# State attention and a gated projection on one core: parity tiles for the scores, and a new order of issue

## The chip, the cores and the metric

The kernel runs on one core of a Trainium2 chip. The core has five engines that each work through their own instructions in order: TensorE (PE in the rows; its weight loads are listed apart as PEld), VectorE (DVE), ScalarE (ACT), GpSimd (POOL) and SyncE (SP), which here issues all DMAs. They meet at semaphores. Matmuls write to PSUM, which this kernel uses as eight banks of 128x512 fp32; everything else lies in SBUF. The metric is the device time of one execution in microseconds.

## The reference

```
# B, H, S, Ns, D = 8, 8, 512, 32, 64; all arrays fp32 (the weights are float64 at the door)
scores  = x @ state.T / sqrt(D)          # (B, H, S, Ns): softmax over the states
xread   = softmax(scores) @ state
scores2 = state @ x.T / sqrt(D)          # (B, H, Ns, S): softmax over the tokens
sread   = softmax(scores2) @ x
seq     = concat([xread, sread], tokens) # (B, S + Ns, H * D)
gate    = sigmoid(causal depthwise conv of seq, 5 taps)
out     = (gate * (seq @ w_val)) @ w_out # (B, 576, 512)
```

Both softmaxes use the same scores, once along the states and once along the tokens.

## The kernel before

There are eight batches. For one batch the kernel loads x, transposes it on PE in four pieces (`xTp`, copied to `xT`), and multiplies with the scaled transposed state: `sc` holds in two PSUM banks, one for each g, the scores of 4 heads by 32 states on the 128 partitions against 512 tokens. DVE transposes `sc` in 32x32 blocks (`scores_T`) and goes on with the softmax over the states there: `max_n`, `sub_n`, `exp_n` on ACT, `sum_n`, `scale_n`, and a transpose back (`probs`). The softmax over the tokens is a max per partition (`max_s`) and an exponential with a summed output on ACT (`exp_s`), transposed on PE (`e2p`) and multiplied with x (`srp`). The probabilities then meet the state twice: `xr` (the read, which only the gate uses; batch 0 does the convolution on PE, the others as taps on DVE) and `val`, the read already multiplied with w_val (`sgv`, split in a high and a low half `swh`, `swl`, as are the probabilities, `ah`, `al`). `g` is gate times value on DVE, split into `gh` and `gl`; `op` is the projection with w_out, 12 matmuls of 128x128x512 for each of four token groups, and `tail` does the 32 state rows of all batches at the end (`tval`, `tacc`, `tg`, `top`). Weights arrive as 64-bit words and are converted by the `words_` functions (`wv`, and `ws_o` for w_out).

Batches 0, 1 and 2 (`LONG`) load x in runs of four tokens, 1 KB at a time: a partition holds tokens 4p to 4p+3 of a head, and a transpose takes two of them at a time, so partitions 0 to 63 of `xT` hold even tokens and 64 to 127 the odd ones behind them, all of one head. For the other batches `xT` holds two heads of the same tokens. Their scores use tiles of 64 rows by 32 columns of the PE array, eight of which lie side by side, with 512 tokens to a matmul. The long-run batches use 128 rows by 32 columns (four tiles), 256 tokens to a matmul: the stationary `sTl` has the state in one half of its rows and zeros in the other (`long_clear`, `long_T`), and writes every other token of one bank.

Nothing is scheduled by the compiler. `ORDER` is a table of step numbers; the steps are listed by `batch`, `group`, `tail` and the lines around them, and issued in the table's order, the letter behind a number choosing ACT, DVE or POOL. Each engine, and SP's queue of DMAs, keeps to it. `warm_up` steps are matmuls whose result nobody reads. Pools hand out buffers in rotation: `sc`, `sgv` and `xr` share four PSUM banks, `val` and `op` two, and the transposes two.

Of the kernel before, what the change touches and what calls it, by code (L numbers as in the profile page):

```python
# [32 lines left out]
37 38v 919 920 921 922 16 17 19 31 48 104 39 52a 115v 40 60a 25 24v 110 108 106 83 33 61a 56 187 111a 55a 109a 21 51a
185 112 113a 54a 116 188 49a 186 26v 34 27 28 85 120 22v 58a 84v 86g 117 57a 62 288 193 66a 287 20a 118 189 194a 121
190a 195 122 124 285 87 125v 67a 89 103 123 191 196a 192a 64a 88 63a 119 126 65 133 77 134a 201 203 127 204 286 139 91
131 197 140a 198 202 132a 128g 130 295 142g 296a 289 141a 135 582 199 290a 90a 92g 216 136 129 217a 293 200 78a 71 205
79 294a 206v 386 93 207 291 143 80v 156 94 292a 101a 81 150 153 99a 144 137 208 184 72a 73 388 297 82 157 301 138a 385
147 298 158a 222 302 148 223a 303 102g 304 209g 74g 299 300 387 224 145 146a 213 225a 159g 168 210 226 164 227 75 97a
211a 169 165 149a 243v 228 212g 230 166a 242 76 214 314 315a 160 268 170a 244 487 215a 229a 245 167g 151 152a 395 389
235 171g 396a 161 486 390a 246 483 95a 231 264 218 247g 237 248 393 232 98g 249 394a 421 162a 219 238 422a 265 239 391  # L40
256 233g 100v 384 316 236v 392a 234 284 317a 423 251 266a 163g 257 220 305 96g 250a 267g 258a 397 318 252 424a 425 253
# [693 lines left out]
```

## Time and profile before

| | before |
|---|---|
| three runs | 247.27, 248.54, 249.08 us (median 248.54) |
| the profiled execution | 247.3 us, of which 245.5 are span |
| PE, DVE, ACT, POOL busy | 94%, 84%, 62%, 52% of the span |
[...]

The span goes from the first instruction to the last. Busy time of PE counts matmuls that overlap one another; how long a group of matmuls really holds PE is read from its start to the start of the next one.

### The profile page before, as it was taken

How to read it: one execution, taken by the hardware profiler on the slowest of the kernel's cores; microseconds unless marked ns; L12 is line 12 of the kernel's file. 1: busy time of each engine (PE TensorE's matmuls, PEld its weight loads, DVE VectorE, ACT ScalarE, POOL GpSimd, SP SyncE). 2: the span in 40 equal slices, each digit the busy share in tenths (PEclk: the TensorE clock that was granted, in tenths of full speed). 3: DMA queues.
4: the chain of work that ended last, by engine and by line, in shares of the span. 5: the costliest groups of instructions: out<-in, count | busy, mean ns of one | idle time of the engine just before them, and what ended most of it. 6: DMA issues, size and time to landing. Idle time of an engine off the chain costs nothing.

```text
span 245.5 us, 5051 instructions
## 1 busy us (share of the span) xinstructions
PE 231.2 (94%) x1955; PEld 167.7 (68%) x1955; DVE 206.3 (84%) x325; ACT 151.0 (62%) x321; POOL 127.0 (52%) x101
## 2 busy tenths in 40 slices
PE   7976999899999999999999999999999999978994
PEld 7953463366677884866787778666766768867882
DVE  3299999999898998899899898998997899987200
ACT  2056977788647875754787769785696475433110
POOL 3001146289959267793575689928758380131200
PEclk9999999999999999999999999999999999999999
DMA  6939987000320309213801021110110302300224
GB/s 194 312 105 341 340 190 169 7 3 0 88 78 10 85 24 277 62 28 88 225 34 53 3 96 62 69 43 3 43 44 3 132 0 85 128 0 3 85 76 138
DMA packets 34549, 22.88 MB, mean 93 GB/s; under 512 B 26058, under 2 KB 29150, under 8 KB 34526
## 3 DMA queue, kind: packets, MB, share of 16 engines
q1 hardware_dynamic: 34526, 22.57, 30.2%
q8 instruction: 15, 0.25, 0.4%
q14 instruction: 8, 0.07, 0.1%
HBM read 13.65 MB, written 8.91 MB: 92 GB/s over the span
## 4 chain that ended last, share of the span: by engine, by line
PE 62%; DVE 24%; DMA 5%; issue 4%; ACT 2%; SPq 1%; DVEq 0%; ACTq 0%
PE val L484 12%; PE op L492 11%; PE op L494 10%; PE op L493 10%; DMA vw<-w_val 4%; PE xTp L309 3%; DVE acc L461 3%; PE xr L421 3%; DVE tacc L518 3%; PE srp L365 3%; DVE g L487 2%; PE e2p L355 2%; PE sgv L287 2%; PE sc L315 2%; DMA ow<-w_out 2%
## 5 line engine op out<-in xcount | busy, mean ns | idle before, releaser
L461 DVE SCALAR_TENSOR_TENSOR acc<-xr,cw,acc 128x509 f32<-128x509 f32 (+2 forms) x84 | 60.6, 739 | 3.8 <-ACT xt L457 2.7
L492 PE MATMUL op<-woh,gh 128*128 128x512 f32 x128 | 52.1, 407 | 1.5 <-DVE g L487 1.1
L494 PE MATMUL op<-woh,gl 128*128 128x512 f32 x128 | 50.4, 394 | 0.0
L493 PE MATMUL op<-wol,gh 128*128 128x512 f32 x128 | 50.1, 392 | 0.0
L175 POOL TENSOR_TENSOR acc<-acc,last 128x508 f32<-128x508 f32 x22 | 28.6, 1304 | 27.6 <-DVE acc L461 22.5
L175 POOL TENSOR_TENSOR gl<-g,gh 128x512 fp32r<-128x512 f32 x25 | 33.0, 1326 | 9.0 <-ACT gh L162 8.4
L492 PEld LDWEIGHTS op<-woh,gh 128*128 128x128 f32 x128 | 24.0, 188 | 13.5 <-DVE g L487 4.0
L162 ACT COPY o<-op 128x512 f32<-128x512 f32 x26 | 15.3, 590 | 21.6 <-PE op L494 21.6
L175 POOL TENSOR_TENSOR ex<-ex,rc 128x1024 f32<-128x1024 f32 x8 | 15.4, 1919 | 25.3 <-DVE rc L406 23.5
L494 PEld LDWEIGHTS op<-woh,gl 128*128 128x128 f32 x128 | 24.0, 188 | 5.4
L493 PEld LDWEIGHTS op<-wol,gh 128*128 128x128 f32 x128 | 24.1, 188 | 4.6
L484 PE MATMUL val<-ah,swh 128*128 128x512 f32 x56 | 24.1, 430 | 1.1 <-DVE g L487 1.1
L473 ACT ACTIVATE sig<-acc 128x512 f32<-128x512 f32 x28 | 17.8, 637 | 9.1 <-POOL acc L175 6.2
L487 DVE SCALAR_TENSOR_TENSOR g<-sig,val 128x512 f32<-128x512 f32 x32 | 21.5, 674 | 2.2 <-PE val L484 1.0
L309 PE MATMUL xTp<-ident,x 128*128 128x128 f32 x128 | 19.2, 279 | 3.7 <-DMA x<-x 2.2
L162 ACT COPY xT<-xTp 128x512 f32<-128x512 f32 x29 | 17.1, 594 | 9.0 <-PE xTp L309 8.8
L484 PE MATMUL val<-ah,swl 128*128 128x512 f32 x56 | 22.1, 395 | 0.0
L484 PE MATMUL val<-al,swh 128*128 128x512 f32 x56 | 22.1, 394 | 0.0
L456 ACT ACTIVATE acc<-xr,cw 128x512 f32<-128x512 f32 x28 | 19.3, 699 | 4.3 <-PE xr L421 3.9
L162 ACT CAST gh<-g 128x512 fp32r<-128x512 f32 x24 | 15.1, 633 | 9.8 <-DVE g L487 9.8
L309 PEld LDWEIGHTS xTp<-ident,x 128*128 128x128 f32 x128 | 14.3, 140 | 9.9 <-issue 1.9
L175 POOL TENSOR_TENSOR al<-sl,ah 128x1024 fp32r<-128x1024 f32 x7 | 17.1, 2443 | 4.5 <-ACT xt L162 3.6
(132 smaller groups left out, 456.3 us busy)
## 6 DMA issues: line engine op xcount, KB each, us to landing
x<-x SPq DMA_DIRECT2D x32, 256.0 KB
out<-o SPq DMA_DIRECT2D x32, 256.0 KB
...
```

Source lines behind the costliest of these rows:

```text
L162: nc.scalar.copy(out, in_)
L175: (nc.vector if e == "DVE" else nc.gpsimd).tensor_tensor(out, a, b, op=how)
L309: nc.tensor.transpose(get("xTp", b, pr)[:, j * P:(j + 1) * P], t, ident)
L365: nc.tensor.matmul(get("srp", b)[NS * q:NS * q + NS, g * D:(g + 1) * D], get("e2T", b, g)[:, j, NS * q:NS * q + NS], heads[:, j, NG * q + ...
L456: nc.scalar.mul(get("acc", b, pr), pt, cw[:, HALO, pr:pr + 1])
L461: nc.vector.scalar_tensor_tensor(acc[:, d:], get("xr", b, pr)[:, :S - d], cw[:, HALO - d, pr:pr + 1], acc[:, d:], op0=ALU.mult, op1=ALU.add)
L473: nc.scalar.activation(get("sig", b, pr), get("acc", b, pr), AF.Tanh, scale=0.5)
L484: nc.tensor.matmul(get("val", b, k), w, a, start=(i == 0), stop=(i == len(parts) - 1))
L487: nc.vector.scalar_tensor_tensor(get("g", b, k), get("sig", b, k), 1.0, get("val", b, k), op0=ALU.add, op1=ALU.mult)
L492: nc.tensor.matmul(pt, gh, woh[:, k], start=(k == 0), stop=False)
L493: nc.tensor.matmul(pt, gh, wol[:, k], start=False, stop=False)
L494: nc.tensor.matmul(pt, gl, woh[:, k], start=False, stop=(k == NPR - 1))
```

## The change

The scores of batches 0 to 2 now use tiles of 64x32. One stationary, `both`, holds the scaled state in both halves of the rows, for all three batches; four instructions fill it (`long_T` over u and t) in place of twelve, and the six `long_clear` memsets are gone. A matmul takes the even or the odd half of `xT` (u) and writes 256 tokens of that parity into a bank of its own, `sc` with index u, in which g now chooses the half. So the max over tokens is taken for each parity and joined (`long_max`, `long_max_both`), each exponential is done in two halves (`long_exp`, twelve in place of six, each with its own sum), the sums are added in `sum_s`, and `probs` becomes four transposes of 256 columns with a step of two (`long_probs`). Sixteen score matmuls to a batch stay sixteen, of 256 tokens each. The whole table `ORDER` is another one, with 58 `warm_up` steps in place of 36.

```diff
@@ -29,40 +29,40 @@
 ORDER = """
-41 50 5 8 0 53 10 107 42v 29 23 43 12 2 44v 11v 6 35 45 18 47 1 30v 13v 32v 14 105 15 915 916 917 918 114 59 3 36v 46
...
+6 23 24g 25 26g 91 41 8 9 5 27 0 43 4 42a 2 10 28 35 7 44v 90 910 911 96 45 93 11v 97v 46 18 47 12 912 913 914 915 916
...
@@ -318,27 +318,22 @@
 
 
 
-    def long_clear(b, u):
-        nc.gpsimd.memset(long_state(b, u)[halves(u)[1]], 0.0)
-
-    def long_state(b, u):
-        return get("sTl", b)[:, u * H * NS:(u + 1) * H * NS].rearrange("p (k u n) -> p k u n", u=2, n=NS)
-
-    def long_T(e, b, u, t):
+    def long_T(e, u, t):
         own, to = halves(u)[0], halves(t)[0]
         scale(
-            e, long_state(b, t)[to, :, u], get("sgp", 0)[own].rearrange("p (k i n) -> p k i n", k=NPR, i=SB)[:, :, b],
+            e, both[to, :, u], get("sgp", 0)[own].rearrange("p (k i n) -> p k i n", k=NPR, i=SB)[:, :, :len(LONG)],
             SCALE)
 
-    def long_scores(b, g):
-        for u in range(2):
+    def long_scores(b):
+        for g in range(NG):
             for q in range(SB):
-                h = NG * q + g
-                nc.tensor.matmul(
-                    get("sc", b, g)[NS * q:NS * q + NS].rearrange("n (p v u) -> n u v p", v=2, u=2)[:, u],
-                    long_state(b, u)[:, h // 2, h % 2],
-                    get("xT", b, h // 2)[:, h % 2 * 256:h % 2 * 256 + 256].rearrange("d (v p) -> d v p", v=2),
-                    start=True, stop=True, tile_position=(0, NS * q))
+                for u in range(2):
+                    r = slice(D * u, D * u + D)
+                    c = slice(g * S // 2, (g + 1) * S // 2)
+                    nc.tensor.matmul(
+                        get("sc", b, u)[NS * q:NS * q + NS, c].rearrange("n (p v) -> n v p", v=2),
+                        both[r, q, g, b], get("xT", b, q)[r, c].rearrange("d (v p) -> d v p", v=2),
+                        start=True, stop=True, tile_position=(D * u, NS * q))
 
 
     def max_s(b, g):
@@ -349,10 +344,27 @@
             get("e2", b, g), get("sc", b, g), AF.Exp, bias=get("nb", b)[:, g:g + 1],
             accum_out=get("sum2", b)[:, g:g + 1])
 
+    def long_max(b, u):
+        nc.vector.tensor_reduce(
+            get("nbl", b)[:, u], get("sc", b, u).rearrange("p (g t) -> p g t", g=NG), axis=AX.X, op=ALU.max,
+            negate=True)
+
+    def long_max_both(b):
+        nc.vector.tensor_tensor(get("nb", b), get("nbl", b)[:, 0], get("nbl", b)[:, 1], op=ALU.min)
+
+    def long_exp(b, g, u):
+        c = slice(g * S // 2, (g + 1) * S // 2)
+        nc.scalar.activation(
+            get("e2", b, g)[:, u * S // 2:(u + 1) * S // 2], get("sc", b, u)[:, c], AF.Exp,
+            bias=get("nb", b)[:, g:g + 1], accum_out=get("suml", b)[:, u, g:g + 1])
+
     def exp_T(b, g):
         for j in range(NJ):
-            t = get("e2", b, g).rearrange("q (p j) -> q j p" if b in LONG else "q (j p) -> q j p", j=NJ)
-            nc.tensor.transpose(get("e2p", b, g)[:, j * P:(j + 1) * P], t[:, j], ident)
+            if b in LONG:
+                t = get("e2", b, g)[:, j % 2 * S // 2:(j % 2 + 1) * S // 2].rearrange("q (p v) -> q v p", v=2)[:, j // 2]
+            else:
+                t = get("e2", b, g)[:, j * P:(j + 1) * P]
+            nc.tensor.transpose(get("e2p", b, g)[:, j * P:(j + 1) * P], t, ident)
 
     def exp_T_copy(e, b, g):
         copy(e, get("e2T", b, g).rearrange("p j q -> p (j q)"), get("e2p", b, g))
@@ -369,7 +381,11 @@
 
     def sum_s(b):
         r2 = get("r2", b)
-        nc.vector.tensor_scalar_add(r2, get("sum2", b), EPS)
+        if b in LONG:
+            both_sums = get("suml", b)
+            nc.vector.scalar_tensor_tensor(r2, both_sums[:, 0], EPS, both_sums[:, 1], op0=ALU.add, op1=ALU.add)
+        else:
+            nc.vector.tensor_scalar_add(r2, get("sum2", b), EPS)
         nc.vector.reciprocal(r2, r2)
 
     def state_read_copy(b):
@@ -407,6 +423,12 @@
 
     def scale_n(e, b):
         combine(e, get("ex", b), get("ex", b), get("rc", b).broadcast_to([P, NB, NS]), ALU.mult)
+
+    def long_probs(b, u):
+        a = get("sl" if b > 0 else "a0", b).rearrange("p g (t u) -> p u g t", u=2)[:, u]
+        ex = get("ex", b).rearrange("p (u g k) n -> p u g (k n)", u=2, g=NG)[:, u]
+        for g in range(NG):
+            nc.vector.transpose(a[:, g], ex[:, g])
 
     def probs(b):
         nc.vector.transpose(get("sl" if b > 0 else "a0", b).rearrange("p g s -> p (g s)"), get("ex", b).rearrange("p k n -> p (k n)"))
@@ -582,11 +604,9 @@
     def group(r):
         op(group_T, r)
         op(state_T, r)
-        for b in LONG if r == 0 else ():
-            for u in range(2):
-                op(long_clear, b, u)
-                for t in range(2):
-                    op(long_T, b, u, t)
+        for u in range(2 if r == 0 else 0):
+            for t in range(2):
+                op(long_T, u, t)
...
@@ -598,20 +618,31 @@
         for pr in range(NPR):
             op(x_T, b, pr)
             op(high, lambda pr=pr: get("xT", b, pr), lambda pr=pr: get("xTp", b, pr))
-        if b not in LONG:
+        if b in LONG:
+            op(long_scores, b)
+            for u in range(2):
+                op(scores_T, b, u)
+                op(long_max, b, u)
+            op(long_max_both, b)
+            for g in range(NG):
+                for u in range(2):
+                    op(long_exp, b, g, u)
+        else:
             op(scores, b)
-        for g in range(NG):
-            if b in LONG:
-                op(long_scores, b, g)
-            op(scores_T, b, g)
-            op(max_s, b, g)
-            op(exp_s, b, g)
+            for g in range(NG):
+                op(scores_T, b, g)
+                op(max_s, b, g)
+                op(exp_s, b, g)
         op(max_n, b)
         op(sub_n, b)
         op(exp_n, b)
         op(sum_n, b)
         op(scale_n, b)
-        op(probs, b)
+        if b in LONG:
+            for u in range(2):
+                op(long_probs, b, u)
+        else:
+            op(probs, b)
         if b > 0:
             op(high, lambda: get("ah", b), lambda: get("sl", b))
             op(low, lambda: get("al", b), lambda: get("sl", b), lambda: get("ah", b))
```

Three places in the program, as the instructions stand on an engine before and now (the number behind a name is a buffer's).

PE, the middle of the scores of batch 0, before:

```order
L337 MATMUL sc_0_240<-xT_0_226,sTl_84 32x2x128
L337 MATMUL sc_0_240<-xT_1_223,sTl_84 32x2x128
L337 MATMUL sc_0_240<-xT_2_237,sTl_84 32x2x128
L337 MATMUL sc_0_240<-xT_3_197,sTl_84 32x2x128
L337 MATMUL sc_1_259<-xT_0_226,sTl_84 32x2x128
L337 MATMUL sc_1_259<-xT_1_223,sTl_84 32x2x128
L337 MATMUL sc_1_259<-xT_2_237,sTl_84 32x2x128
L337 MATMUL sc_1_259<-xT_3_197,sTl_84 32x2x128
```

and now:

```order
L333 MATMUL sc_0_255<-xT_0_196,both 32x2x128
L333 MATMUL sc_1_257<-xT_0_196,both 32x2x128
L333 MATMUL sc_0_255<-xT_1_145,both 32x2x128
L333 MATMUL sc_1_257<-xT_1_145,both 32x2x128
L333 MATMUL sc_0_255<-xT_2_247,both 32x2x128
L333 MATMUL sc_1_257<-xT_2_247,both 32x2x128
L333 MATMUL sc_0_255<-xT_3_228,both 32x2x128
L333 MATMUL sc_1_257<-xT_3_228,both 32x2x128
```

Eight matmuls for one bank followed eight for the other, four to each padded stationary; now the matmuls of the two parities alternate between the two banks.

SP's queue at the start of the program (vw is w_val, ow w_out, cww the convolution, sg a group of states, x_98 and x_93 batch 0), before:

```order
L199 DMA vw_3_82<-w_val 128x512
L203 DMA cww<-conv_w 20x128
L186 DMA x_98<-x 128x2x256
L199 DMA vw_1_102<-w_val 128x512
L199 DMA vw_0_104<-w_val 128x512
L199 DMA vw_2_119<-w_val 128x512
L270 DMA sg_123<-state 32x8x64 x4
L186 DMA x_98<-x 128x2x256 x3
L199 DMA ow_2_216<-w_out 128x512
L186 DMA x_221<-x 128x2x256 x4
```

and now:

```order
L199 DMA vw_0_86<-w_val 128x512
L186 DMA x_93<-x 128x2x256
L199 DMA vw_3_95<-w_val 128x512
L203 DMA cww<-conv_w 20x128
L199 DMA vw_2_123<-w_val 128x512
L186 DMA x_93<-x 128x2x256 x2
L270 DMA sg_149<-state 32x8x64 x4
L186 DMA x_93<-x 128x2x256
L199 DMA vw_1_226<-w_val 128x512
L199 DMA ow_1_243<-w_out 128x512
L186 DMA x_282<-x 128x2x256 x4
L186 DMA x_322<-x 128x2x256 x4
```

Batch 0 and the states now go ahead of the last piece of w_val, and the first piece of w_out ahead of batch 1. On DVE the same stretch, before, at the first scores:

```order
L231 SCALAR_TENSOR_TENSOR wv<-vw_0_104,ws_v_201 128x512
L216 TENSOR_SCALAR ws_o_257<-ow_2_216 128x512
L164 COPY cwb<-cwbp_228 128x128
L172 TENSOR_SCALAR wc_o_270<-ow_2_216 128x512
L388 STREAM_TRANSPOSE sl_273<-sc_0_240 128x512
L345 TENSOR_REDUCE nb_288<-sc_0_240 128x1
L388 STREAM_TRANSPOSE sl_273<-sc_1_259 128x512
L345 TENSOR_REDUCE nb_288<-sc_1_259 128x1
L394 TENSOR_REDUCE mx_306<-sl_273 128x32
L226 SCALAR_TENSOR_TENSOR ws_o_257<-wc_o_270,ws_o_257 128x512
L175 TENSOR_TENSOR sl_273<-sl_273,mx_306 128x1024
```

and now:

```order
L172 TENSOR_SCALAR both<-sgp_219 64x4x96 x2
L216 TENSOR_SCALAR ws_v_245<-vw_1_226 128x512
L221 TENSOR_SCALAR wc_v_273<-wc_v_273 128x512
L226 SCALAR_TENSOR_TENSOR ws_v_245<-wc_v_273,ws_v_245 128x512
L348 TENSOR_REDUCE nbl_290<-sc_0_255 128x2
L216 TENSOR_SCALAR ws_o_293<-ow_1_243 128x512
L404 STREAM_TRANSPOSE sl_295<-sc_0_255 128x512
L348 TENSOR_REDUCE nbl_290<-sc_1_257 128x2
L404 STREAM_TRANSPOSE sl_295<-sc_1_257 128x512
L353 TENSOR_TENSOR nb_325<-nbl_290 128x2
L226 SCALAR_TENSOR_TENSOR ws_o_293<-wc_o_276,ws_o_293 128x512
L410 TENSOR_REDUCE mx_367<-sl_295 128x32
```

The first scores are taken up when three of the four pieces of w_val have been converted, and the last piece and w_out come in between them.

DVE at the end of the program, before:

```order
L175 TENSOR_TENSOR xtl<-xt,xth 128x1024
L175 TENSOR_TENSOR gl_1_2738<-g_1_2631,gh_1_2700 128x512
L175 TENSOR_TENSOR gl_3_2754<-g_3_2654,gh_3_2694 128x512
L461 SCALAR_TENSOR_TENSOR acc_0_2610<-xr_0_2474,cw,acc_0_2610 128x509
L518 SCALAR_TENSOR_TENSOR tacc_2687<-xt,cw,tacc_2687 128x256 x4
L487 SCALAR_TENSOR_TENSOR g_2_2779<-sig_2_2744,val_2_2747 128x512
L518 SCALAR_TENSOR_TENSOR tacc_2781<-xt,cw,tacc_2781 128x256 x4
L487 SCALAR_TENSOR_TENSOR g_0_2800<-sig_0_2790,val_0_2783 128x512
L175 TENSOR_TENSOR gl_0_2830<-g_0_2800,gh_0_2802 128x512
L548 SCALAR_TENSOR_TENSOR tg_2833<-tsig_2777,tval_2764 128x512
```

and now:

```order
L509 SCALAR_TENSOR_TENSOR g_1_2760<-sig_1_2735,val_1_2725 128x512
L175 TENSOR_TENSOR xtl<-xt,xth 128x1024
L509 SCALAR_TENSOR_TENSOR g_0_2782<-sig_0_2745,val_0_2764 128x512
L164 CAST gh_0_2787<-g_0_2782 128x512
L509 SCALAR_TENSOR_TENSOR g_3_2790<-sig_3_2737,val_3_2775 128x512
L540 SCALAR_TENSOR_TENSOR tacc_2743<-xt,cw,tacc_2743 128x256 x8
L540 SCALAR_TENSOR_TENSOR tacc_2733<-xt,cw,tacc_2733 128x256 x4
L175 TENSOR_TENSOR gl_0_2861<-g_0_2782,gh_0_2787 128x512
L570 SCALAR_TENSOR_TENSOR tg_2865<-tsig_2863,tval_2807 128x512
L540 SCALAR_TENSOR_TENSOR tacc_2733<-xt,cw,tacc_2733 128x256 x4
L570 SCALAR_TENSOR_TENSOR tg_2891<-tsig_2888,tval_2831 128x512
```

The last two products g of batch 7, which stood between the taps `tacc` of the tail, now stand ahead of all of them; its last `gl` stands behind twelve of the sixteen taps. On PE the 48 `tval` matmuls, which stood in three pieces among `val` and `op`, stand together behind the last `val`.

## Rows read from the trace of the kernel before

**Rows 1.** The page, its first part: busy time, share of the span, and count of PE, DVE, ACT and POOL.

```profile
PE 231.2 (94%) x1955; PEld 167.7 (68%) x1955; DVE 206.3 (84%) x325; ACT 151.0 (62%) x321; POOL 127.0 (52%) x101
```

**Rows 2.** Busy time of the engines by stretch of the span: the stretch, its length, then PE, PEld, DVE, ACT, POOL with counts, clock, DMA share and GB/s.

```profile
12.00:48.00 36.00, 30.92 (x367) 17.06 (x370) 35.02 (x60) 26.93 (x62) 10.71 (x10) 1.00 0.69 198
95.00:194.00 99.00, 98.99 (x908) 71.48 (x907) 90.73 (x136) 71.47 (x153) 69.90 (x49) 1.00 0.23 70
208.00:245.50 37.50, 31.44 (x157) 25.98 (x155) 18.79 (x30) 9.25 (x17) 5.26 (x4) 1.00 0.21 73
```

**Rows 3.** The chain of waits in order of time (start us, us, what): the read of batch 1, the first projection, the first and last of three pieces of fillers in the middle, and the copy of the last projection.

```profile
47.89 1.47 PE xr L421 x15
...
63.97 0.43 PE op L492
...
101.41 0.45 PE warm L243 x4
...
141.33 0.45 PE warm L243 x4
...
241.95 0.59 ACT o L162
```

**Rows 4.** The timeline of PE: the scores of batch 2 in tiles of 128x32, of batch 3 in tiles of 64x32, and what follows each (start us, us, engine, line, operation, xcount).

```profile
40.26 1.93 PE L337 MATMUL sc<-xT,sTl 128*32 128x256 f32 x32
42.13 1.09 PE L287 MATMUL sgv<-wv,sT 64*32 64x512 f32 x16
...
61.85 1.09 PE L315 MATMUL sc<-xT,sT 64*32 64x512 f32 x16
62.87 1.10 PE L365 MATMUL srp<-x,e2T 128*32 128x64 f32 x64
```

**Rows 5.** The timeline of PE around a group of small tiles that stands alone between projections, and four transposes with what follows them.

```profile
66.54 0.40 PE L494 MATMUL op<-woh,gl 128*128 128x512 f32 x1
66.87 1.09 PE L287 MATMUL sgv<-wv,sT 64*32 64x512 f32 x16
67.89 0.50 PE L492 MATMUL op<-woh,gh 128*128 128x512 f32 x1
68.22 0.40 PE L493 MATMUL op<-wol,gh 128*128 128x512 f32 x1
...
79.82 0.60 PE L309 MATMUL xTp<-ident,x 128*128 128x128 f32 x4
80.18 0.47 PE L484 MATMUL val<-ah,swh 128*128 128x512 f32 x1
```

**Rows 6.** The timeline of PE and DVE in the start-up: when the second and the fourth-issued piece of w_val have landed, the first scores, and DVE's first work on them.

```profile
8.95 0.43 DVE L172 TENSOR_SCALAR wc_v<-vw 128x512 f32<-128x512 f32 x1 [2.48 <-DMA vw<-w_val]
12.32 0.43 DVE L172 TENSOR_SCALAR wc_v<-vw 128x512 f32<-128x512 f32 x1 [1.97 <-DMA vw<-w_val]
...
17.28 2.67 PE L337 MATMUL sc<-xT,sTl 128*32 128x256 f32 x32
...
21.07 0.71 DVE L388 STREAM_TRANSPOSE sl<-sc 128x512 f32<-128x512 f32 x1
```

**Rows 7.** The chain of waits, DVE in the start-up, and one tap of the gate later; its instructions follow without a gap there, so that the second number is what one of them holds DVE for.

```profile
20.82 0.33 DVE wc_o L172
21.15 0.62 DVE sl L388
21.77 0.58 DVE nb L345
...
23.55 1.12 DVE mx L394
24.67 0.60 DVE ws_o L226
...
27.61 1.23 DVE sm L404
...
32.34 1.15 DVE a L412
...
81.58 0.66 DVE acc L461
```

**Rows 8.** Groups of instructions by line and shape: busy us, mean ns of one, idle time before them.

```profile
L175 POOL TENSOR_TENSOR gl<-g,gh 128x512 fp32r<-128x512 f32 x25 | 33.0, 1326 | 9.0 <-ACT gh L162 8.4 <-PE sc L315 0.5
L162 ACT CAST gh<-g 128x512 fp32r<-128x512 f32 x24 | 15.1, 633 | 9.8 <-DVE g L487 9.8
L348 ACT ACTIVATE e<-sc,nb 128x512 f32<-128x512 f32 x16 | 11.0, 689 | 2.7 <-DVE nb L345 2.7
L518 DVE SCALAR_TENSOR_TENSOR tacc<-xt,cw,tacc 128x256 f32<-128x256 f32 x16 | 10.4, 651 | 0.9 <-ACT tacc L512 0.5
```

**Rows 9.** The timeline of PE at the end: its three waits in the tail (in brackets the idle time ahead, and what ended it).

```profile
217.36 0.51 PE L484 MATMUL val<-ah,swh 128*128 128x512 f32 x1 [0.88 <-DVE g L487]
...
221.63 0.39 PE L544 MATMUL tval<-xth,wvh 128*128 128x256 f32 x1 [1.17 <-DVE g L487]
...
223.70 0.47 PE L492 MATMUL op<-woh,gh 128*128 128x512 f32 x1 [0.38 <-DVE tg L548]
```

**Rows 10.** The timeline, the last product g of batch 3 on DVE, and the first matmul that reads its low half.

```profile
122.92 0.68 DVE L487 SCALAR_TENSOR_TENSOR g<-sig,val 128x512 f32<-128x512 f32 x1
...
135.71 0.39 PE L494 MATMUL op<-woh,gl 128*128 128x512 f32 x1
```

More of the change, by code (lines that the diff above doesn't have):

```diff
@@ L31 @@
 ORDER = """
-41 50 5 8 0 53 10 107 42v 29 23 43 12 2 44v 11v 6 35 45 18 47 1 30v 13v 32v 14 105 15 915 916 917 918 114 59 3 36v 46
[L33 to L41, printed above, removed]
@@ new lines @@
+655v 719 799g 803 721 740 610 722 741v 800 703g 720a 664 573 723 665a 666 742 611 881g 804 743 726 728 729 673 874a
+801a 744 724g 674a 876g 759 747 730 725 802v 812 567 748 705 749v 805a 704 727a 733 675 745g 735 815v 731g 806 879g
+670 706a 746 813a 736 612 732 760 671a 613a 814 751 734v 737 709 750g 816 752 761v 738g 817 753a 832 826a 834 762g 570
+839 739 818 755 835 756 667 754g 807a 668v 833a 808 757a 854 836 672 841 669 809 810 842 758g 769 837g 710 820 843
+811v 838 855 840a 825 856a 711 712a 844g 819a 827 770a 828 857g 829 830v 875g 772 773a 850 821 894 831 845 822 882a
@@ L66 @@
+823v 885 824 766 851 767a 846 883v 852g 858 847 853g 771 848v 884 859 877g 774 763 889 764a 887 886 768 899 895 890
+896 849v 888 891 576 900 860a 861g 897 898 765 901 865 902v 866a 867 862 892a 871 863a 872a 873 893v 903v 907 904 908v
+864 868 909 869a 905v 906 1 870
 """.split()
@@ L121, in state_attention_gated_kernel @@
     alias = dict(
-        wc=("g", F32), ws=("o", I32), sTl=("last", F32), z5=("zc", F32), vw0=("al", I32), vw1=("swl", I32), ow0=("al", I32), ow1=("swl", I32),
+        wc=("g", F32), ws=("o", I32), z5=("zc", F32), vw0=("al", I32), vw1=("swl", I32), ow0=("al", I32), ow1=("swl", I32),
         sg=("acc", F32), a0=("ah", F32), sw0=("swh", F32),
@@ L148, in state_attention_gated_kernel @@
         ("cw", [P, TAPS, NPR], F32), ("ones", [P, 2], F32),
-        ("sel", [TAPS * NPR, TAPS, P], F32), ("cwb", [P, TAPS, P], F32),
+        ("both", [P, NPR, 2, len(LONG), NS], F32), ("sel", [TAPS * NPR, TAPS, P], F32), ("cwb", [P, TAPS, P], F32),
         ("z", [P, B, NG, D], F32), ("xt", [P, NPR, B, HALO + NS], F32),
@@ L152, in state_attention_gated_kernel @@
         fixed[name,] = const.tile(shape, dt, name=name)
-    ident, wv, woh, wol, cw, ones, sel, cwb, z, xt = (
-        fixed[n,] for n in ("ident", "wv", "woh", "wol", "cw", "ones", "sel", "cwb", "z", "xt"))
+    ident, wv, woh, wol, cw, ones, both, sel, cwb, z, xt = (
+        fixed[n,] for n in ("ident", "wv", "woh", "wol", "cw", "ones", "both", "sel", "cwb", "z", "xt"))
     def two(t):
```

51 lines of the change are left out of this document (26 added, 25 removed).

## The prediction

> **What bounds the kernel now.** I began with the page: PE is busy for 94% of the span and DVE for 84% [rows 1], and the granted clock is full throughout, so nothing here is about the clock. An average hides the stages, so the stretches came next. From 12 to 48 us DVE is busy for 35.0 of 36.0 us; from 95 to 194 us PE is busy for 98.99 of 99.00; in the last 37.5 us PE loses 6.1 [rows 2]. The chain of waits shows where the one bound gives way to the other: at 47.89 it passes to PE with the read of batch 1 [rows 3], which had waited for that batch's probabilities on DVE. So the end is the time at which batch 1's read starts, plus PE's work behind it, plus what PE still waits, plus 3.6 us from the copy of the last projection, at 241.95 [rows 3], to the end of the span. The profiled execution took 247.3 us with a span of 245.5; it is the lowest of the three runs, 1.2 us under their median. I make the sum against 247.3.
>
> **The score tiles.** Each fp32 matmul stands twice in the trace. A batch of scores in 128x32 tiles holds PE from 40.26 to 42.13, 1.87 us for 32 rows on four tiles, eight rounds of 256 columns; in 64x32 tiles batch 3 takes 61.85 to 62.87, 1.02 us for two rounds of 512 on eight tiles [rows 4]. The new form has 32 rows on eight tiles, four rounds of 256: the same columns as the latter, so 1.0 us. Bounds: 0.9 (half of 1.87) and 1.87 (the two row halves do not overlap). I take 1.0, since its tile is that of the 1.02 row. The saving, 3 x 0.87 = 2.6 us, lies wholly ahead of batch 1's read, where PE has time to spare, so it counts only through the delay of batch 0's scores.
> [...] The old tiles write every fourth column or so of a bank and still take 0.23 us for 256 columns, against 0.51 for 512 contiguous ones [rows 4], so a step costs nothing that shows. [...] And the 32 rows of 128x32 tiles in 1.87 us leave 58 ns to each, so the old form alone can't tell whether the issue of a matmul or its columns took the time; the 16 rows of 1.02 us (64 ns each) can't either. [...]
>
> **The start-up.** The second piece of w_val (1.33 MB deep in SP's queue: pieces of w_val have 0.52 MB, of x 0.26, the four of a state group 0.26, cww 0.02) is used at 8.95 us and the last-issued (2.38 MB deep) at 12.32 [rows 6], so data arrive at 0.31 MB a us. Batch 0's last piece of x was 3.43 MB deep in the queue and is 2.90 now: 1.7 us earlier, about 14.0 us. Its transposes (0.4), a copy (0.6) and the scores (1.0, after four scalings of `both` on two engines in place of twelve on one) put the end of the scores near 16.5. Before, they began at 17.28, ended near 19.95, and DVE came to them at 21.07 [rows 6].
> From there to batch 1's probabilities the new order has, on DVE, 6 maxima at 0.60, 6 transposes of scores at 0.62, 3 `mx` at 1.13, 2 sums with their reciprocals at 1.73, 4 + 5 conversions (L226, L231) at 0.60, 6 short ones at 0.33, 2 `g` at 0.60, 0.7 of small ones [rows 7], and 8 transposes of 256 columns. For those: the forms of 512 and 1024 columns differ by 0.53 (0.62, 1.15), so 256 columns take 0.09 + 0.26 = 0.35, together 2.8; bounds 0.31 each (half of 0.62) and, if the output's step of two halves the rate, 0.62. Sum 26.2 us. Waits, estimated: the scores of batch 1 about 1.0, the exponential of batch 0 behind four half exponentials on ACT about 1.5 (689 ns for a whole one [rows 8]), and 1.0 for the rest. So 16.6 + 26.2 + 3.5 = 46.3, against 47.9: **-1.6**. Bounds: no waits (42.8, -5.1), and no gain (0).
>
> **Behind batch 1's read.** I counted PE's work in both orders from there to the end, each group at its start-to-start time: a projection's matmul at 0.23, a group of small tiles at 1.02, four transposes at 0.36 [rows 4, 5]. Before 184.4 us, now 180.2. Of the 4.2 us, 3.0 are moved ahead into PE's spare time: batch 1's `srp` (1.0), two `val` of batch 0 (0.9), two `e2p` (0.7), the second group's transposes (0.4). The other 1.2 is the grouping: going into small tiles costs 0.10 (0.33 in place of 0.23 from 66.54) and coming out 0.10 (0.33 from 67.89) [rows 5]; before there are 22 such excursions, now 16. **-4.2**; bounds -3.0 and -4.6.
> Three pairs of fillers in the middle, 0.45 us each [rows 3], have no counterpart: **-1.3** if nothing else is late there.
> In place of `e2p` and two `val` of batch 0, batch 1's `val` follows its read closely, and needs `al`, which stands on DVE behind two `swl`, a `g` and itself (0.6 x 3 + 1.1). Read and `halo` end 1.3 us after the read starts: **+1.5**, bounds 0 and 2.
>
> **The tail.** PE idles there 0.88 + 1.17 + 0.38 = 2.4 us, each time for a product that DVE makes between or behind the taps `tacc` [rows 9]. Now all `tval` come behind the last `val` and the `op` between, 8.4 us of PE, in which DVE has two `g`, a `gh`, twelve taps at 0.65 [rows 8] and the last `gl`: 10.1 us. A wait of 1.7 replaces 2.4: **-0.7**, bounds -2.4 and +1.
>
> **Costed at nothing.** The max over two banks, its join, and twelve half exponentials lie on DVE and ACT beside PE's fillers; DVE's total changes by about -1 us, POOL's by +5 at 52% busy [rows 1]. If DVE became the bound this cover would be gone; that is the third rival.
>
> **The sum.** -1.6 - 4.2 - 1.3 + 1.5 - 0.7 = -6.3, so 247.3 - 6.3 = **241.0 us**. All bounds at their best (-5.1, -4.6, -1.3, 0, -2.4) give -13.4, 233.9; at their worst (0, -3.0, 0, +2, +1) 247.3.
>
> **Rivals.**
> *More of the start-up is gained (0.12).* DVE's waits fall into the conversions and the new `val` wait vanishes: 3.5 + 1.5 less, 236.0. For it: DVE was idle for only 1.0 of 36 us there before [rows 2]. Against: POOL and ACT have more to do in it now.
> *The tiles gain nothing (0.05).* The scores stay at 1.9 us; batch 0's cost 1 us on the path: 242.0.
> *The lead is used up (0.18).* The first projection of a batch needs its four `g`. I added DVE's steps [rows 7] up to the `g` that is latest against its use, and took off PE's up to the projection: for batches 0 to 7 +3.0, +5.6, +0.3, -3.9, -5.5, -2.5, -6.0, -1.8 before, and +5.3, +6.7, +4.0, +5.4, +1.8, +2.0, -1.9, -9.4 now. Batch 3's last product was ready at 123.60 and its low half read at 135.71 [rows 10], 12.1 us ahead; that lead falls by 9.3, to some 3, of which `gh` (0.63) and `gl` (1.33) take 2 [rows 8]. If batches 3, 4 and 5 each wait 1.5 us: 241.0 + 4.5 = 245.5.
> *DVE and POOL are late at every projection, slower (0.10).* The same place, but the lag grows: it decides when DVE loses more than 1 us to a batch beyond what it lost before, as a conversion beside POOL does, and batches 2 to 7 then wait 2 us each: 241.0 + 12 = 253.0. For it: seven of the eight lags have risen, and POOL has more to do. Against: DVE's work is 84% of the span, and before it never held PE longer than a few tenths between 95 and 194 us [rows 2].
>
> **The numbers.** The forecast, 241.0, has 0.55. One per cent, 2.5 us, is what a measurement of this kernel can tell from no change; below 246.1 is faster. Forecast, the first two rivals and a third of the next are faster: 0.78; the rest of the lead's case and the low end of the last are within 1%, 0.13; slower 0.09. The range leaves out half of the last rival and the far ends: 234.5 to 247.
>
> **What would show it.** The 32 rows of scores within 1.0 to 1.1 us; batch 1's read near 46; the first projection near 56 (63.97 before [rows 3]); no fillers behind 30 us; about 16 small groups that PE enters alone, with 0.33 at each end; one wait of 1 to 2 us behind `tval`. It would be wrong if PE shows waits for `g`, `gl` or `al` in the stretch from 95 to 194 us, or if batch 1's read comes at 48 or later.

## The result: 0.9% slower, and where the forecast time went

The changed kernel takes 249.6 us (median of 22 runs, 248.9 to 251.6); beside it the kernel before takes 247.8 (22 runs). The ratio is 1.0087, with a 95% interval of 1.0064 to 1.0110. The forecast of 241.0 was wrong, and the time lies above its range. The profiled execution took 250.1 us with a span of 248.2, 2.7 more than the span before. Runs of the kernel before fall into two groups 1.3 to 2.2 us apart, with a mean granted clock of 1.00 and of 0.986 (246.1 and 247.6 us beside runs 1 to 4), and every ratio here is to both groups together: to the runs at 1.00 alone most would be 0.002 to 0.004 higher.

| | before | forecast | after |
|---|---|---|---|
| read of batch 1 | 47.9 | 46.3 | 50.6 |
| first projection | 64.0 | 56 | 61.4 |
| from batch 1's read to the last copy `o` | 194.1 | 189.4 | 193.9 |

The last row of the forecast is 194.1 - 4.2 - 1.3 + 1.5 - 0.7. The start-up lost 2.7 us instead of gaining 1.6, and behind it only 0.1 of the 4.7 forecast was gained.

The changed kernel's page (its line for [rows 1]) and busy time by stretch (for [rows 2]; PE, PEld, DVE, ACT, POOL with counts, clock, DMA share, GB/s):

```profile
PE 233.3 (94%) x1999; PEld 170.7 (69%) x1999; DVE 213.1 (86%) x331; ACT 149.0 (60%) x323; POOL 138.6 (56%) x103
```

```profile
12.00:48.00 36.00, 33.02 (x476) 22.07 (x475) 32.67 (x62) 25.61 (x63) 11.37 (x8) 1.00 0.71 204
95.00:194.00 99.00, 94.41 (x739) 67.12 (x727) 94.02 (x135) 63.59 (x134) 71.03 (x48) 1.00 0.19 59
208.00:248.20 40.20, 35.77 (x178) 29.37 (x176) 23.27 (x36) 12.03 (x23) 8.99 (x7) 1.00 0.20 72
```

From 12 to 48 us DVE now idles 3.3 us where it idled 1.0. From 95 to 194 PE, which missed 0.01 us, misses 4.6, and DVE is busy for 3.3 more. DVE's total rose by 6.8 us.

**The start-up** (for [rows 6]), from the timeline of PE and DVE:

```profile
13.26 1.95 PE L243 MATMUL warm<-ident 128*128 128x128 f32 x16
...
15.14 1.15 PE L259 MATMUL cwbp<-cwf,sel 20*128 20x128 f32 x8
16.14 0.18 PE L247 MATMUL cwp<-ident,cwf 20*128 20x20 f32 x1
16.25 0.66 PE L276 MATMUL sgp<-ident,sg 128*128 128x128 f32 x4
16.37 0.18 DVE L250 COPY cw<-cwp 128x20 f32<-128x20 f32 x1 [2.21 <-PE cwp L247]
16.46 0.68 DVE L226 SCALAR_TENSOR_TENSOR ws_v<-wc_v,ws_v 128x512 int32<-128x512 int32 x1
...
17.18 0.69 DVE L231 SCALAR_TENSOR_TENSOR wv<-vw,ws_v 128x512 int32<-128x512 int32 x1
17.97 1.12 DVE L172 TENSOR_SCALAR both<-sgp 64x384 f32<-64x384 f32 x2
...
19.14 1.10 PE L333 MATMUL sc<-xT,both 64*32 64x256 f32 x32 [0.91 <-DVE both L172]
...
20.86 0.68 DVE L348 TENSOR_REDUCE nbl<-sc 128x2 f32<-128x512 f32 x1
```

The state group's transposes `sgp` stand in PE's queue behind fillers and the convolution's matmuls. DVE idles 2.21 us for the latter and then makes a piece of `wv` ahead of `both`, for which the scores wait. They begin at 19.14, 1.9 us later than before.

**Batch 1's read and the first projection** (for [rows 3]), from the timeline of PE:

```profile
29.45 1.15 PE L309 MATMUL xTp<-ident,x 128*128 128x128 f32 x8 [1.62 <-ACT xT L162]
...
50.62 0.65 PE L443 MATMUL xr<-sl,z 32*64 32x512 f32 x3
...
52.39 0.50 PE L506 MATMUL val<-ah,swh 128*128 128x512 f32 x1
53.76 0.51 PE L506 MATMUL val<-al,swh 128*128 128x512 f32 x1 [0.87 <-DVE al L175]
...
61.44 0.50 PE L514 MATMUL op<-woh,gh 128*128 128x512 f32 x1 [0.43 <-DVE g L509]
```

Before, the read waited 0.82 us for batch 1's probabilities on DVE:

```profile
47.89 1.47 PE L421 MATMUL xr<-sl,z 32*64 32x512 f32 x16 [0.82 <-DVE sl L412]
```

Now it waits for nothing but PE itself. The probabilities were ready at 49.97, and PE has no wait from 29.45 to the read: 21.2 us of matmuls one behind the other, among them what was moved ahead of the read.

**The tiles and a lone small group** (for [rows 4, 5]), from the timeline of PE:

```profile
33.54 1.09 PE L333 MATMUL sc<-xT,both 64*32 64x256 f32 x32
34.57 0.74 PE L367 MATMUL e2p<-ident,e 128*128 128x128 f32 x4
...
67.28 0.40 PE L516 MATMUL op<-woh,gl 128*128 128x512 f32 x1
67.60 0.66 PE L315 MATMUL sc<-xT,sT 64*32 64x512 f32 x8
```

The 32 rows of scores take 1.03 us, as forecast, where they took 1.87. The step into a small group is 0.32.

**The middle.** PE's waits from 60 to 200 us by what ended them (us in total, times, longest):

```profile
PE val L506 <- DVE g L509: 1.9, 2, 1.6
PE val L506 <- ACT o L162: 1.3, 1, 1.3
PE op L514 <- DVE g L509: 1.3, 2, 0.8
PE op L516 <- POOL gl L175: 0.6, 1, 0.6
```

Six waits on three engines, 5.1 us. They stand at 61 (the first projection), 129 and 154, and three of them, 3.7 us, at 184 to 194.

**DVE beside POOL** (for [rows 8]): groups by shape (busy us, mean ns | idle before), and four rows of the timeline of POOL and DVE.

```profile
L175 DVE TENSOR_TENSOR gl<-g,gh 128x512 fp32r<-128x512 f32 x6 | 10.2, 1708 | 0.5 <-POOL gh L166 0.3 <-ACT gh L162 0.2
L175 DVE TENSOR_TENSOR al<-sl,ah 128x1024 fp32r<-128x1024 f32 x2 | 3.9, 1956 | 0.0
```

```profile
173.86 1.92 POOL L175 TENSOR_TENSOR ex<-ex,rc 128x1024 f32<-128x1024 f32 x1 [3.72 <-ACT gh L162]
173.89 2.43 DVE L175 TENSOR_TENSOR gl<-g,gh 128x512 fp32r<-128x512 f32 x1 [0.17 <-ACT gh L162]
175.74 2.88 POOL L175 TENSOR_TENSOR al<-sl,ah 128x1024 fp32r<-128x1024 f32 x1
176.25 2.39 DVE L388 TENSOR_SCALAR r<-sum 128x2 f32<-128x2 f32 x1
```

The `gl` that began 0.03 us behind POOL's `ex` ends 0.54 us behind its end; `r`, two numbers to a partition, lasts until POOL's `al` is done. The same `gl` took 829 ns in the mean before (7 of them); six cost 5.3 us more now than at that mean.

**The tail** (for [rows 9]): two waits, 1.4 us, where there were three of 2.4.

```profile
227.05 0.50 PE L514 MATMUL op<-woh,gh 128*128 128x512 f32 x1 [1.05 <-DVE tg L570]
...
230.45 0.51 PE L514 MATMUL op<-woh,gh 128*128 128x512 f32 x1 [0.37 <-DVE tg L570]
```

### The profile page after: what moved, and what is told of

Its sections match the earlier page's. It is cut to its first block, busy times and chain, and to the rows that moved or that the text cites. A ratio compares the mean times of both kernels' runs of the same rounds, so it can differ in the third digit from the quotient of the medians.

```text
span 248.2 us, 5148 instructions
## 1 busy us (share of the span) xinstructions
PE 233.3 (94%) x1999; PEld 170.7 (69%) x1999; DVE 213.1 (86%) x331; ACT 149.0 (60%) x323; POOL 138.6 (56%) x103
## 4 chain that ended last, share of the span: by engine, by line
PE 48%; DVE 32%; POOL 9%; ACT 5%; issue 4%; DMA 1%; SPq 0%; DVEq 0%; POOLq 0%; ACTq 0%
PE val L506 11%; PE op L514 7%; PE op L516 7%; PE op L515 7%; PE warm L243 5%; DVE acc L483 4%; DVE tacc L540 3%; DVE g L509 3%; PE xTp L309 3%; DVE sl L404 2%; DVE gl L175 2%; DVE mx L410 2%; POOL gl L175 2%; POOL sl L175 2%; PE xr L443 2%
## 5 line engine op out<-in xcount | busy, mean ns | idle before, releaser
L175 POOL TENSOR_TENSOR gl<-g,gh 128x512 fp32r<-128x512 f32 x26 | 34.3, 1326 | 15.4 <-ACT gh L162 14.7
L175 POOL TENSOR_TENSOR acc<-acc,last 128x508 f32<-128x508 f32 x22 | 29.4, 1338 | 18.7 <-DVE acc L483 9.9
L162 ACT COPY o<-op 128x512 f32<-128x512 f32 x27 | 15.9, 589 | 26.5 <-PE op L516 11.8
L175 POOL TENSOR_TENSOR sl<-sl,mx 128x1024 f32<-128x1024 f32 x8 | 16.2, 2020 | 8.0 <-DVE mx L410 7.9
L162 ACT COPY xT<-xTp 128x512 f32<-128x512 f32 x28 | 15.9, 592 | 7.4 <-PE xTp L309 7.4
L309 PE MATMUL xTp<-ident,x 128*128 128x128 f32 x128 | 18.5, 276 | 2.0 <-ACT xT L162 1.9
L170 ACT ACTIVATE last<-xr,cw 128x508 f32<-128x508 f32 x21 | 14.5, 694 | 9.1 <-DVE acc L483 8.9
```

Of the source, the lines that this page charges most:

```text
L162: nc.scalar.copy(out, in_)
L170: nc.scalar.mul(out, in_, factor)
L175: (nc.vector if e == "DVE" else nc.gpsimd).tensor_tensor(out, a, b, op=how)
L309: nc.tensor.transpose(get("xTp", b, pr)[:, j * P:(j + 1) * P], t, ident)
```

## The experiments

Theory A: the loss is the start-up's order. Theory B: it is single waits behind the first projection, each made by where one step stands or on which engine. Theory C: the tiles gain and the order gives it back. Numbers in the diffs are entries of `ORDER`. Ratios are to the kernel before on the same chip.

### 1. The start-up's order

```diff
-95v 36a 920 921 922 923 19 16 48 38g 92 29 101v 20a 17 98 39 40 51a 53a 52v 50v 63 31 99a
+95v 36a 38g 92 29 101v 48 51a 53a 52v 50v 98 99a 19 16 20a 17 39 40 63 31
```

> The changed kernel with its start-up put in another order: the four transposes of the first group of states (sgp), the four `both` copies and the last x transposes of batch 0 stand ahead of the convolution weights' matmuls, and four fillers go. Theory A (the start-up was late because sgp stood behind fillers and the convolution's matmuls, and DVE idled 2.2 us there): scores of batch 0 begin at 15.9 us (19.14 in the changed kernel), the read of batch 1 at about 48.3 (50.62), the first projection at about 59 (61.44), and the run takes 247.2 us, 2.4 below the changed kernel. Rival (DVE and POOL are the bound in the middle, so a lead from the start is used up there): the start moves as said, the first projection is at 59, and the run still takes 249 to 250 us, with more waits of PE on g, gl or al behind 95 us.

Ratio 1.0074 (1.0047 to 1.0102); in the trace the read of batch 1 comes at 49.3, the first projection at 60.1, the end 1.4 us earlier. The timeline:

```profile
17.10 1.09 PE L333 MATMUL sc<-xT,both 64*32 64x256 f32 x32
...
19.56 0.68 DVE L348 TENSOR_REDUCE nbl<-sc 128x2 f32<-128x512 f32 x1
```

In the two traces the lead is carried to the end, but it is 1.4 us and not 2.4: six instructions for `w_val` and `cw` fill DVE from 16.33 to 19.56, and the maxima wait behind them. Its size is uncertain. Runs 2 and 9 have the changed kernel's own start-up and read batch 1 at 50.4 and 49.7 us, so one and the same order differs by almost 1 us from trace to trace; the ratios, 1.0074 and 1.0087, are not apart by more than their intervals. Theory A holds in the traces, for some 1 us.

### 2. Thirteen instructions from DVE to ACT

```diff
-324v 331v 430v 543v 642v 741v 734v 508v 609v 464v 749v 761v 848v
+324a 331a 430a 543a 642a 741a 734a 508a 609a 464a 749a 761a 848a
```

> The changed kernel with 13 instructions of batches 2 to 7 given from DVE to ACT: 7 gate_last, 2 copies of e2T, 4 casts gh (about 9 us of DVE's work, of which ACT, busy 60%, has room). Theory B (in the middle DVE is the bound: it is busy 94 of 99 us between 95 and 194 us, and PE's waits there end on it): DVE's busy time there falls to about 88 us, PE's waits of 4.6 us between 95 and 194 fall to 1.5, and the run takes 246.5 us. Rival (the waits come from where the steps stand in the queues and from POOL, not from the amount of DVE's work): 249.0 to 250.5, or slower where ACT's queue is now late with an o copy or a gate.

Ratio 1.0098 (1.0060 to 1.0136): nothing gained. The stretch from 95 to 194, and the two largest waits of PE from 60 to 200:

```profile
95.00:194.00 99.00, 96.12 (x749) 68.49 (x748) 88.08 (x128) 69.49 (x148) 71.25 (x49) 1.00 0.19 59
```

```profile
PE e2p L367 <- ACT e2T L162: 1.5, 1, 1.5
PE op L514 <- ACT o L162: 1.3, 1, 1.3
```

DVE does fall to 88.08 us, as asked for, and PE's waits only from 5.1 to 4.5: new ones end on ACT, whose queue has a `gh` or a `last`, itself waiting for DVE, ahead of the copy that PE needs. So it is not the amount of DVE's work alone.

### 3 and 8. The new tiles in the old order

```diff
-long_scores 0 0 ... scores_T, max_s, exp_s ... long_scores 0 1 ... probs 0
+long_scores 0 ... long_max 0 0, long_max 0 1, long_max_both 0, scores_T, long_exp ... long_probs 0 0, long_probs 0 1
```

> The new score tiles and their softmax path in the order and with the engines of the kernel before: each old score step is replaced by the new one at its place, the zeroing of the padded states and eight of their twelve copies are gone. Theory C (the tiles are a gain of their own, and the new order gives it back): PE's scores of the three batches take 3.1 us in all rather than 5.6, ACT and POOL have less ahead of batch 0's scores, and the run takes 245.0 us, 2.8 below the kernel before. Rival (the tiles give nothing, since DVE's chain sets the start-up and the two halves of maxima, exps and four transposes of probs lengthen it): 247.5 to 249, with the read of batch 1 at 47.9 or later.

Ratio 1.0052 (1.0023 to 1.0081): theory C falls. In the trace the read of batch 1 comes at 48.0 (47.9 before), the first projection at 64.6 (63.97), and all that follows keeps this 0.7 us. 2.5 us of PE's work are gone and no stage is earlier.

The eighth kernel takes the third's subtractions `113v` and `197v` to POOL (`113g`, `197g`).

> The new tiles in the order of the kernel before (the third kernel) with the subtraction of the maximum of batches 0 and 1 on POOL rather than DVE: 2 x 1.21 us less for DVE in the start-up, and 2 x 0.8 us longer from one step to the next, since POOL takes 2.0. Theory D (DVE's amount of work until the first projection sets it): the read of batch 1 is 1.5 to 2.4 us earlier than the third kernel's 48.0, and the ratio to the kernel before falls from 1.005 to 0.997. Rival (the chain of the softmax's steps sets it, not DVE's amount): no change or 1 to 2 us later, ratio 1.005 to 1.012.

Ratio 1.0056 (1.0025 to 1.0088), as the third's, so the rival holds: less DVE work with longer steps gains nothing. The read of batch 1 comes at 48.9 in its trace, but the mean granted clock of that execution is 0.979 (1.00 in the third's profiled one), so the 0.9 us need not be the steps'.

### 4 and 5. Start-up and letters together, then five letters by the waits left

The fourth kernel is the first and the second together.

> The edits of the first two together. If A and B both hold and add up: 244.2 us. If the start's lead is what the middle uses up unless DVE is relieved: 244 to 245, though the first alone gains nothing. If neither: 249 to 250.

Ratio 1.0024 (1.0000 to 1.0048). The fifth sets five more letters:

```diff
-324a 331a 749a 452g 563g
+324v 331v 749v 452a 563a
```

> The fourth kernel (new start-up order and DVE's work given to ACT) with five letters set by its own waits: two gate_last of batch 2 and the cast gh of batch 6's first channel go back to DVE (ACT was late there: PE waited 1.6 us at 81.6 for an o copy and 1.8 at 186 for an e2T copy), and the casts gh of batch 3's and batch 4's POOL go to ACT (PE waited 1.0 us at 128.3 for POOL's gl and 0.7 at 153.2). Theory B (what is left behind the first projection are single waits, each from one engine's queue): the four waits of 5.1 us go, some come back at other places, and the run takes 3 us less than the fourth kernel, 243.3 on the chip of the first four runs, 1.2% below the kernel before. Rival (one wait removed only shows the next, since DVE is the bound): no more than 1 us below the fourth kernel.

Ratio 0.9873 (0.9821 to 0.9925), 1.3% faster than the kernel before. Its stretch, and its waits from 60 to 200:

```profile
95.00:194.00 99.00, 97.03 (x770) 70.07 (x755) 88.77 (x132) 70.72 (x150) 71.43 (x48) 1.00 0.19 62
```

```profile
PE val L506 <- DVE g L509: 1.8, 2, 1.6
PE op L514 <- DVE g L509: 0.4, 1, 0.4
PE xTp L309 <- ACT xT L162: 0.2, 1, 0.2
```

Five letters bring 1.5%, and DVE's busy time is that of the second kernel (88.8 against 88.1). Theory B holds: with the same amount of work on DVE, the place of five steps decides. Whether they would have gained as much without the first thirteen was not run. The longest wait for a `g`, 1.6 us, is still there.

### 9. The letters alone

The fifth kernel's letters with the changed kernel's start-up.

> The fifth kernel's letters (13 given from DVE to ACT, of which three went back, and two casts gh from POOL to ACT) with the changed kernel's own start-up. Theory B (the loss of the changed kernel lies mostly in single waits behind the first projection, cured by letters alone; the start-up's order is worth 1.4 us, as the first kernel's trace had it): first projection at 61.3, last projection at 239.4, ratio to the kernel before 0.993. Rival (the start-up is the larger part of the loss): ratio 1.000 or more.

Ratio 0.9887 (0.9848 to 0.9926). From its first projection to batch 5's it takes 112.3 us (113.9 in the changed kernel), from there to batch 6's 26.3 (29.3). These 4.6 us lay behind the start-up, and letters alone give them back.

### 6, 10 and 11. More score work

```diff
-102 ... 186 ... 289
+102 102 ... 186 186 ... 289 289
```

> The changed kernel with the 32 score matmuls of each of batches 0, 1 and 2 issued twice in a row: 3 x 1.03 = 3.1 us more of PE's work, all of it ahead of the first projection. Theory D (until the first projection DVE's chain is the bound, and PE's time there is free, so what the new tiles save there was never on the path): the ratio to the kernel before stays at 1.009 (no more than 0.4 us more). Rival (PE's work counts, as the prediction had it for the scores behind the first ones): 2 to 3.1 us more, ratio 1.017 to 1.021.

Ratio 1.0135 (1.0084 to 1.0186) against 1.0087: 0 to 2.6 us more, and the first projection at 61.2 in the trace (61.4 without). It decides nothing; so the places were parted, on the fifth kernel: `289` four times, then `102` and `186` twice.

> The fifth kernel (ratio 0.987) with batch 2's 32 score matmuls issued four times in a row: 3 x 1.03 = 3.1 us more of PE's work at 32.6 us, the output unchanged. Theory E (until some 28 us PE waits for the softmaxes of batches 0 and 1, from there on PE itself is the bound, so that PE's work counts only from there): 2.5 to 3.1 us more, ratio 0.997 to 1.000, all of it before the first projection. Rival D (PE's time is free until the first projection): no more than 0.5 us, ratio 0.987 to 0.989.

> The fifth kernel with the score matmuls of batches 0 and 1 issued twice: 2 x 1.03 = 2.1 us more of PE's work, at 16.6 and 20.9 us. Theory E (before 28 us PE's time is free): no more than 0.5 us, ratio 0.987 to 0.989. Rival (PE's work counts everywhere, or the second pass holds up DVE's maxima): 1 to 2.1 us more, ratio 0.991 to 0.996.

Ratios 0.9949 (0.9923 to 0.9975) and 0.9834 (0.9797 to 0.9871). The timelines of the tenth and of the eleventh:

```profile
32.09 3.68 PE L333 MATMUL sc<-xT,both 64*32 64x256 f32 x128
...
62.15 0.50 PE L514 MATMUL op<-woh,gh 128*128 128x512 f32 x1 [0.42 <-DVE g L509]
```

```profile
16.99 1.96 PE L333 MATMUL sc<-xT,both 64*32 64x256 f32 x64
...
60.02 0.50 PE L514 MATMUL op<-woh,gh 128*128 128x512 f32 x1 [0.43 <-DVE g L509]
```

Twice the scores of batches 0 and 1 cost nothing. Four times batch 2's are 2.6 us more work (3.6 us to the next start, 1.03 of them the first pass) and put the first projection 2.0 us later than the fifth kernel's 60.1 (1.9 by the ratios). The missing half microsecond is no slack, since PE lost time in the fifth kernel's trace at a lower granted clock (0.91 in the mean from 28 to 48 us, where run 10's whole execution has 1.00):

```profile
27.01 1.14 PE L309 MATMUL xTp<-ident,x 128*128 128x128 f32 x8 [1.62 <-ACT xT L162]
...
32.62 1.09 PE L333 MATMUL sc<-xT,both 64*32 64x256 f32 x32
```

From that wait to batch 2's scores it takes 5.6 us there and 4.1 in run 10. From PE's last wait ahead of it the read of batch 1 comes 21.2 us later in the changed kernel and in runs 1, 4 and 11, and 23.7 in run 10 (28.0 to 51.7), without a wait between: 2.6 us, all of the added work. So PE's time is free ahead of some 28 us and counts in full from there on. Theory E holds.

### 7. Less DVE work in the start-up

`w_out` is joined without its low words and not scaled back, so that the product is not the reference's.

```diff
-65 67 71 73 77 59 61 79
+
-    ... hi, SIGN, get("ws", *key)[:p, :n], ...
+    ... hi, SIGN, get("wc", *key)[:p, :n].bitcast(I32) if key[0] == "o" else get("ws", *key)[:p, :n], ...
```

> The changed kernel without eight of the DVE instructions that turn w_out's words into f32 (the shift of the low word and the join of it, 4 x 0.42 + 4 x 0.68 = 4.4 us, between 21 and 45 us; the product uses a w_out that is not scaled back). Theory D (DVE is the bound until the first projection): the read of batch 1 comes at 46.2 rather than 50.6, the first projection at 57, and the run takes 4 us less than the changed kernel, ratio to the kernel before 0.992. Rival (the start-up is bound by transfers or PE): the read of batch 1 within 1 us of 50.6 and the ratio at 1.007 or more.

Ratio 1.0066 (1.0035 to 1.0098). The read of batch 1 comes at 49.0, 1.6 us earlier, for 4.4 us of work taken out; 0.7 of it is there already at the first scores (18.4 us), up to which the two orders are the same. DVE's timeline shows why it is so little:

```profile
43.36 0.69 DVE L510 SCALAR_TENSOR_TENSOR g<-sig,val 128x512 f32<-128x512 f32 x1 [1.34 <-ACT sig L475]
```

DVE, freed, waits for `sig`, which waits for PE's read of batch 0. Batch 1's probabilities are ready at 47.1, 1.9 us ahead of the read, and PE again has no wait from 27.9 us to it, 21.2 us. So the start-up is a chain over several engines up to some 28 us, and PE's own work from there on. How much of it could be shortened stays open.

### 12. What was left of the waits

```diff
-204v (al of batch 1) ... 849v behind the tail taps, 860a behind the first tail gate
+204g ... 859 849g 860a
```

> The fifth kernel with what is left of its waits taken up: al of batch 1 on POOL rather than DVE, where it took 2.29 us and stood ahead of g and of the taps (PE waits 1.1 us on it at 51.1 and 0.4 for g at 60.1); in the tail gl of batch 7's first channel on POOL rather than behind the 12 tail taps on DVE, and the cast gh of its last channel ahead of the first tail gate on ACT (PE waits 1.1 us at 219.8 and 0.5 at 223.6). Theory B: 1 to 2.5 us less than the fifth kernel, ratio 0.977 to 0.983. Rival: al on POOL holds up wol, which the first projection needs, by 2.5 us, and gives back what the tail brings: ratio 0.986 to 0.990.

Ratio 0.9958 (0.9923 to 0.9994): 2 us lost against the fifth kernel. The timelines of DVE and POOL, and a stretch:

```profile
57.34 4.11 DVE L175 TENSOR_TENSOR acc<-acc,last 128x508 f32<-128x508 f32 x1
...
55.25 2.54 POOL L175 TENSOR_TENSOR wol<-ws_o,woh 128x512 fp32r<-128x512 f32 x2
57.73 1.31 POOL L175 TENSOR_TENSOR acc<-acc,last 128x508 f32<-128x508 f32 x1
58.98 1.93 POOL L175 TENSOR_TENSOR sl<-sl,mx 128x1024 f32<-128x1024 f32 x1
```

```profile
63.00:67.00 4.00, 3.99 (x11) 3.18 (x12) 3.93 (x7) 3.69 (x7) 1.14 (x2) 0.59 0.00 0
```

With `al` on POOL, POOL's work moves later and a DVE add that took 0.68 us in the fifth kernel lasts through POOL's `wol`, `acc` and `sl`, 4.11 us. PE waits 2.88 us for a `g`, and the first projection comes at 63.0, 2.9 us later than the fifth kernel's. In this execution, of 248.3 us, PE then loses 1.4 us more at the lower clock; the 2 us of the ratios are covered without it. The tail's two edits gain nothing (its waits come to 1.6 us, 1.3 in the fifth kernel). It is worse than the rival had it, and for another cause.

### 13. The old tiles in the tuned order

The score tiles, copies, zeroing and softmax path of the kernel before, each in the place of the new step in the fifth kernel's order.

```diff
-long_scores 0 ... long_max 0 0, long_max 0 1, long_max_both 0 ... long_probs 0 0, long_probs 0 1
+long_scores 0 0, long_scores 0 1, long_T 1 ... max_s 0 0, max_s 0 1 ... probs 0
```

> The score tiles, the twelve copies, the zeroing and the undivided softmax path of the kernel before, in the fifth kernel's order and with its engines: each new score step is replaced by the old one at its place, the extra copies stand on ACT behind the scores of the batch before. It tells what the tiles are worth once the waits are gone; the regrouped order stays. Theory E (PE's time counts only from some 28 us on: batch 2's scores, 0.84 us longer, count in part, those of batches 0 and 1 do not, and DVE's shorter path of 0.7 us is given back): 0 to 1 us more than the fifth kernel, ratio 0.987 to 0.991. Rival (the tiles carry the gain: 2.5 us of PE's work and eight copies on ACT come back on the path): 2.5 to 4 us more, ratio 0.997 to 1.003.

Ratio 0.9853 (0.9815 to 0.9891), as the fifth kernel's. The timeline of PE:

```profile
27.78 1.15 PE L309 MATMUL xTp<-ident,x 128*128 128x128 f32 x8 [0.47 <-ACT xT L162]
...
31.88 1.93 PE L337 MATMUL sc<-xT,sTl 128*32 128x256 f32 x32
...
60.27 0.51 PE L492 MATMUL op<-woh,gh 128*128 128x512 f32 x1 [0.41 <-DVE g L487]
```

The scores take 1.86 us again and every stage from batch 1's read on comes within 0.2 us of the fifth kernel, whose trace has the 1.5 us lost to the clock in it. Counted from PE's last wait at 27.78, the read at 49.8 is 22.0 us away in place of 21.2: batch 2's old tiles do cost their 0.85 us there, and those of batches 0 and 1 nothing. So in the old order the tiles are worth nothing that shows, and in the new one under 1 us, which the totals can't tell; the order without them is 1.5% faster than the kernel before, once its waits are gone.

## Why the prediction was wrong, step by step

- **The score tiles, 1.0 us: right** (1.03). The next step, that their saving "lies wholly ahead of batch 1's read, where PE has time to spare", holds in the old order (run 3) and for batches 0 and 1 (run 11). It fails for batch 2, behind whose scores PE has no time to spare in the new order (runs 10 and 13). That the saving counts "through the delay of batch 0's scores" fails too: twice those scores cost nothing in run 11. The rival "the tiles gain nothing" named the wrong cause, scores that stay at 1.9 us: writing every second column costs nothing that shows (1.03 us, beside 1.02 for the contiguous ones of batch 3 [rows 4]), and 64 rows start within 1.89 us in run 6, 30 ns to a row and 59 to a matmul, so the old form's 58 to a row were not the time to issue one; the 64 rows of `srp` stand at 17 and 34 [rows 4].
- **The start-up, -1.6: wrong, +2.7.** The sum of DVE's steps held: from the first maximum to batch 1's probabilities it took 29.1 us, and the step had 29.7. What failed is its start, "the end of the scores near 16.5". It was reckoned from when data land, and not from what stands ahead in the queues of PE (16 rows of fillers, the convolution) and DVE (`cw`, `wv`); it was 20.2. Run 1 undoes 2.0 us of these 3.7, and 1.3 of it reaches the read. The model of the stage was incomplete as well: the read followed the probabilities by 0.65 us, behind PE's own work, into which 3.0 us had been moved as if into spare time.
- **Behind batch 1's read, -4.2: right for the work, which was not the time.** The fifth kernel covers the way from the read to the last `o` copy in 188.8 us, 5.2 less than before; the terms behind the read came to 4.7. PE is busy for 184.1 us of them, 6.1 less than before, where work and fillers were to give 5.5 (the counts 184.4 and 180.2 are some 4 us low, nearly alike). In the changed kernel, waits ate all of it. Grouping was not tested by itself; its rows agree (0.32 at a lone group's entry).
- **The fillers, -1.3: gone as said, but "if nothing else is late there" did not hold.** This is the step that failed most: 5.1 us of waits from 60 to 200.
- **The new wait for `al`, +1.5: right within its bounds** (1.37 from 52.39 to 53.76 in place of 0.23, so 1.1). **The tail, -0.7: right** (1.0).
- **"DVE's total changes by about -1 us": wrong, +6.8.** Durations were taken from the trace before, where `gl` took 0.83 us in the mean. Now `gl` takes 1.71, four of the six beside POOL, which is 5.3 us more in all; the two `al` took 1.96 in the mean where 1.1 was reckoned; `gh` and `r` are longer too (692 and 831 ns in the mean, before 418 and 482). The four rows at 174 us show two that last until POOL's is done, and run 12's add of 4.11 us is a third. The trace before had the like: the conversion `ws_o` that began at 40.22 us, 0.05 behind POOL's `ex`, took 2.41, where two others of its form took 0.68.
- **The rival "the lead is used up" was the right one behind the read, with a chance of 0.18.** Both signs that the prediction names for being wrong came: PE waits for `g` and `gl` between 95 and 194 us, and a read of batch 1 at 48 or later. The rival priced three waits of 1.5 us at batches 3 to 5. They were 1.0 and 0.7 (start to start) at batches 3 and 4, and 3.7 us at 184 to 194. Its count of lags summed DVE alone; of these waits one ended on an `o` copy behind casts in ACT's queue and one on POOL's `gl`.

So two terms failed: the start of the start-up, 4.3 us, and the waits behind batch 1's read, 4.6 (193.94 - 189.36). With 241.0 they make 249.9; the profiled execution took 250.1.
